# Windowed attention and a gated layer on one core: queries loaded a token to a partition and transposed by transfers, half a tile per step

## The chip, the cores and the metric

The kernel runs on one core of a Trainium2 chip. A core has a matrix engine (TensorE, in the profile PE, with its weight loads as PEld), a vector engine (DVE), a scalar engine (ACT), a general engine (GpSimd, POOL) and a sync engine (SP) that mainly issues transfers. Each engine works through its own instructions in the order of the program and waits on semaphores for the others. Transfers (DMA) are issued from the queues of SP, ACT and POOL and run on sixteen DMA engines. The metric is the device time of one execution in microseconds, as the median of several; less is better.

## The reference

```python
# q, k, v: (8, 8, 576, 64) float32 = batch, heads, tokens, head size
scores = (1 / sqrt(64)) * q @ k.T                 # per batch and head
mask   = abs(pos_q - pos_k) <= 32                 # within one batch entry
attn   = softmax(where(mask, scores, -1e9))
x      = (attn @ v) -> (4608 tokens, 512)         # heads side by side
h      = x @ w_in                                 # 512 -> 2048
g      = h * sigmoid(1.702 * h)
out    = g @ w_out                                # 2048 -> 512, float32
```

## The kernel before

The 8 x 576 tokens are treated as one row of 4608. Attention runs over 36 units of 128 queries: unit u holds the queries 128u+32 to 128u+159, in two blocks of 64, and each block sees 128 keys that start 32 tokens before it. The two layers run over 18 tiles of 256 tokens (two units). `head` starts up and works on tokens 0 to 1535; after it `window(w)` is called for w = 4 to 19. A window w computes the attention of units 2w and 2w+1, the first layer of tile w-1 (eight steps of eight matmuls, `layer1`), and the second layer of tile w-2 by seven products of 2x2 blocks (`product`). The order of all instructions on every engine is written out by hand.

Scores need keys and queries with the head dimension on the partitions. They stand in `kT` and `qT`, rings of 1536 tokens, of which each tile of 512 tokens (0 to 8) fills a third. A few tokens behind the end of each ring repeat its beginning, so that a block that crosses the end can be read in one piece. Tiles get into the rings in several ways:

- Tiles A (320 tokens) and B (256), 1, 2 and 3: `load_heads` loads four consecutive tokens of a head to a partition (256 numbers in a row). `pair_heads` copies them on DVE or POOL so that two heads stand side by side, TensorE transposes them through PSUM (`heads_T`, L176 and L179), and DVE (keys, `keys_T`) or ACT (queries, `queries_T`) copies the result to the ring (L106).
- Keys of tiles 4 to 8: `load_keys` (L146) loads one token to a partition (rows of 64 numbers), and `keys_X` (L151) writes the ring by a transposing transfer on SP, 128 tokens each.
- Queries of tiles 4 to 8: `load_heads` as above, four copies on DVE (`pair_heads`), and one transposing transfer for all 512 tokens (`queries_X`, L221).

Because of the four tokens to a partition, `qT` keeps queries in the order (token modulo 4, token divided by 4). A block of 64 queries is therefore four runs of 16, and the exponential (L269) writes its 64 results back in natural order.

The loads are issued on POOL's queue (they cast float32 to bf16). In `window`, `loads()` comes first: two loads of values `ve` (L157), which wait until the buffers of eight units earlier are free, and in even windows the keys and queries of tile w/2+3. `feed(w)` comes near the end: the shifted values `vo` (`odd_v`), and the transposing transfers; in even windows the first half of the keys of tile w/2+2, in odd ones the queries and the second half of the keys of tile (w+4)/2 rounded down. On SP's queue they stand between the stores of the output (L423, L349) and the transposing transfers of the attention's result, `x_T` to `xT` (L315), which the first layer of the next window reads. In window 4 TensorE transposes tile 3 between the last four steps of `layer1`; this is the only window in which it transposes keys or queries.

The casting loads of POOL and the transfers of SP each cycle through eight semaphores. A transfer that takes a semaphore again waits until the one before it on that semaphore has landed, so at most eight loads and eight SP transfers are under way.

Of the kernel before, what the change touches and what calls it, by code (L numbers as in the profile page):

```python
# [16 lines left out]
BF16 = mybir.dt.bfloat16  # L17
# [7 lines left out]
RING = 1536  # L25
RP = RING // JT


class _Kernel:
# [37 lines left out]
    def setup(self):  # L67
        nc, cst = self.nc, self.cst
        self.ident = cst.tile([128, 128], BF16, name="ident")
        self.mask = cst.tile([128, 4, SQ], BF16, name="mask")  # L70
        self.w_in_sb = cst.tile([128, self.NK, self.DFF], BF16, name="w_in_sb")
        self.w_out_sb = cst.tile([128, self.NFF, self.DM], F16, name="w_out_sb")
        self.w_sum = cst.tile([128, 4, self.NFF // 2, self.DM // 2], F16, name="w_sum")
        self.kT = cst.tile([128, 4, RING + 64], BF16, name="kT")
        self.qT = cst.tile([128, 4 * JT, RP + 16], BF16, name="qT")
        self.k_first = cst.tile([128, 4, 64], BF16, name="k_first")
        self.q_first = cst.tile([128, 4 * JT, 8], BF16, name="q_first")
        self.ve = [cst.tile([128, self.H, 66], BF16, name=f"ve{i}") for i in range(NV)]
        self.vo = [cst.tile([128, self.H, 66], BF16, name=f"vo{i}") for i in range(NV)]
        self.v_first = cst.tile([64, self.H, 66], BF16, name="v_first")  # L80
        self.idle = cst.tile([128, 512], BF16, name="idle")
        nc.vector.memset(self.idle, 0.0)
        self.spark = cst.tile([128, 1], F32, name="spark")
        nc.vector.memset(self.spark, 0.0)
        make_identity(nc, self.ident)
        for i in range(NV):
            nc.vector.memset(self.ve[i][:, :, self.D:], 1.0)
# [52 lines left out]

    def load_keys(self, i):

        kn = self.stage["k", i] = self.work.tile([128, JT, self.H, self.D], BF16, name="ks", tag="ks", bufs=3)
        for c in range(JT):
            for off, b, s, n in self.pieces(512 * i + 128 * c, 128):
                self.nc.gpsimd.dma_start(kn[off:off + n, c], self.k[b, :, s:s + n, :].rearrange("h s d -> s h d"))  # L146

    def keys_X(self, i, c):

        at = (512 * i + 128 * c) % RING  # L150
        self.nc.sync.dma_start_transpose(self.kT[:, :, at:at + 128],  # L151
                                         self.stage["k", i][:, c].rearrange("p h d -> p (h d)"))

# [28 lines left out]

    def keys_T(self, i, hp, kind="t", eng=None):
        tp = self.heads_T("k", i, hp, kind)
        lo, size = self.tokens(i)
        at = lo % RING

        def put(dst, n):
            self.cast(eng or self.nc.vector, dst.rearrange("r (p j) -> r p j", j=JT),
                      tp[:, :, :n // JT].rearrange("r j p -> r p j"))  # L190

        put(self.kT[:, hp, at:at + size], size)
        if at == 0 and lo:
            put(self.kT[:, hp, RING:], 64)

    def queries_T(self, i, hp, kind="t", eng=None):
        lo, size = self.tokens(i)
        at, n = lo // JT % RP, size // JT
        tp = self.heads_T("q", i, hp, kind)
        self.cast(eng or nc.vector, self.qT[:, JT * hp:JT * hp + JT, at:at + n], tp[:, :, :n])  # L200

# [16 lines left out]

    def queries_X(self, i):
        at = (128 * i) % RP  # L220
        self.nc.sync.dma_start_transpose(self.qT[:, :, at:at + 128],  # L221
                                         self.stage["q", i, "c"].rearrange("p h j t d -> p (h j t d)"))

    def queries_wrap(self, i):
        if (128 * i) % RP == 0:
            self.nc.vector.tensor_copy(self.qT[:, :, RP:RP + 8] if i else self.q_first, self.qT[:, :, 0:8])

    def setup_neg(self):

        pool = self.nc.gpsimd  # L230
        self.neg = self.cst.tile([128, 2, SQ], BF16, name="neg")
        pool.memset(self.neg, 0.0)
        for b in range(2):
            for half in range(2):
                sign = 1 if half == b else -1
                ap = self.neg[64 * half:64 * half + 64, b, :].rearrange("k (j s) -> k j s", j=JT)
                pool.affine_select(out=ap, in_=ap, compare_op=ALU.is_ge, fill=-30000.0, base=0,  # L237
                                   pattern=[[-sign, JT], [-sign * JT, SQ // JT]], channel_multiplier=sign)

# [8 lines left out]
    def scores(self, u):  # L248
# [6 lines left out]
        for hp in range(4):  # L255
            for blk in range(2):
                k0 = (128 * u + 64 * blk) % RING
                q0 = (128 * u + 64 * blk + 32) % RING // JT
                for half in range(2):
                    lo, at = 64 * half, k0 + 64 * (half ^ blk)  # L260
                    for eo in range(2):
                        r = slice(eo * 64, eo * 64 + 64)
                        nc.tensor.matmul(sc[eo][lo:lo + 64, 2 * hp + blk, :], self.kT[r, hp, at:at + 64],  # L263
                                         self.qT[r, JT * hp:JT * hp + JT, q0:q0 + 16], start=(seen and n == 0),
                                         stop=(n == 7), skip_group_check=not seen)
                n += 1
        p = self.work.tile([128, 2, 8, SQ], BF16, name="p", tag="p", bufs=5)
        for eo in range(2):
            nc.scalar.activation(p[:, eo].rearrange("k h (s j) -> k h s j", j=JT),  # L269
                                 sc[eo].rearrange("k h (j s) -> k h s j", j=JT), AF.Exp, scale=self.scale)  # L270
        self.p[u] = p
# [168 lines left out]
    def head(self):  # L440
# [37 lines left out]
        for hp in range(4):  # L478
            self.keys_T("A", hp, "ht"[hp % 2], dve)
            self.queries_T("A", hp, "ho"[hp % 2], act)  # L480
            if hp < 2:
                self.blind(hp)
# [21 lines left out]
        for hp in range(4):  # L504
            self.keys_T("B", hp, "htho"[hp], dve)
            if hp < 2:
                self.pair_heads("q", "B", hp + 2, dve)
            self.queries_T("B", hp, "hoth"[hp], act)
        self.scores(2)
# [14 lines left out]
        dve.tensor_copy(self.k_first, self.kT[:, :, 0:64])  # L524
        self.queries_wrap(0)
        for n in range(4):
# [13 lines left out]
        for hp in range(4):  # L540
            self.keys_T(1, hp, "a", dve)
            self.queries_T(1, hp, "a", act)
            run(1)
# [27 lines left out]
        for c in "kq":  # L571
            self.load_heads(3, c)
        self.layer1(2, 0)
# [8 lines left out]
        for hp in range(4):  # L582
            self.keys_T(2, hp, "t", dve)
            if hp in (1, 2):
                self.w_sums(hp + 1, 1)
            self.queries_T(2, hp, "o", act)
            self.layer1(2, 4 + hp)
        for m in (7, 8, 9):
            self.odd_v(m, dve)
        for m in (11, 12, 13):  # L590
            self.load_v(m)
        self.load_keys(4)
        self.load_heads(4, "q")

    def window(self, w):
# [10 lines left out]
        def loads():  # L606
            for m in (2 * w + 6, 2 * w + 7):
                if m < self.NU:
                    self.load_v(m)
            if w % 2 == 0 and 512 * (w // 2 + 3) < self.N:  # L610
                self.load_keys(w // 2 + 3)
                self.load_heads(w // 2 + 3, "q")

        if w == 4:
# [9 lines left out]
            self.gelu_table()  # L624
            for m in (10, 11):
                self.odd_v(m, act)
            self.band(b)
# [11 lines left out]
            loads()  # L639
            run(l1, 2)  # L640
            for c in "qk":
                for hp in range(4):
                    self.pair_heads(c, 3, hp, dve)
            run(l1, 2)
            for hp in range(4):
                self.keys_T(3, hp)
                self.queries_T(3, hp, "a", nc.scalar)
                run(l1)
            self.g_sums(w - 1, 0)
# [79 lines left out]
    def feed(self, w):  # L729

        dve = self.nc.vector
        if w % 2 == 0:
            self.queries_wrap((w + 2) // 2)
        for m in (2 * w + 2, 2 * w + 3):
            if 11 < m < self.NU:
                self.odd_v(m, dve)
        i = (w + 4) // 2
        if 512 * i < self.N:
            if w % 2:
                if 512 * i % RING == 0:  # L740
                    dve.tensor_copy(self.kT[:, :, RING:], self.kT[:, :, 0:64])
                for hp in range(4):
                    self.pair_heads("q", i, hp, dve)
                self.queries_X(i)
            for c in ((2, 3) if w % 2 else (0, 1)):
                self.keys_X(i, c)
        if w == 16:
            dve.tensor_copy(self.kT[:, :, RING:], self.k_first)
            dve.tensor_copy(self.qT[:, :, RP:RP + 8], self.q_first)

# [51 lines left out]
```

## Time and profile before

| | |
|---|---|
| time, median of 8 runs | 299.08 us (295.73 to 302.59) |
| the profiled execution | 296.16 us, of which its span is 294.0 us |
| granted clock of TensorE | 0.999 |
| packets of the casting loads (software queue) | 75,888, 18.16 MB |
| packets of SP's queue | 42,272, 18.62 MB |
| packets under 512 B, of all 118,649 | 96,080 |
| POOL's issues of query loads | 17, of 64 to 512 KB |
| POOL's issues of key loads | 30, most of 128 KB |
| SP's transposing transfers | 28 to `xT`, 20 to `kT`, 5 to `qT` |

Lines of the profile read `line engine operation out<-in shapes xcount | busy us, mean ns | idle before`. Lines of the timeline read `start us, us, engine line operation xcount [idle before <- what ended it]`; consecutive alike instructions are merged, and a q behind an engine's name means its queue (an issue or a wait, during which the engine itself does nothing). "DMA to landing" is the time from the issue of a transfer to the semaphore that tells of its end.

### The profile page before, as it was taken

Reading aid. Unit: us, or ns where it says so; the run is one execution under the profiler, and the core shown is the slowest. Engines: PE = TensorE matmul, PEld = TensorE weight load, DVE = VectorE, ACT = ScalarE, POOL = GpSimd, SP = SyncE. Lnnn points to the kernel's source line nnn. Section 1 sums busy time; section 2 is a strip of 40 time slices with the busy share of each in tenths; the row PEclk is TensorE's granted clock in tenths of the full one; section 3 lists DMA queues with packets and bytes.
Section 4 is the critical chain, followed back from the end, with each engine's and each line's share of the span. In section 5 each row is a group of like instructions: output and inputs, shape, how many; then the busy total and the mean of one; then the engine's idle time right before and its main releaser. Section 6 shows DMA issues by size and latency. Waiting matters only on the chain.

```text
span 294.0 us, 9589 instructions
## 1 busy us (share of the span) xinstructions
PE 287.4 (98%) x4052; PEld 236.4 (80%) x4052; DVE 193.8 (66%) x584; ACT 189.6 (64%) x314; POOL 87.3 (30%) x127
## 2 busy tenths in 40 slices
PE   8999999999999999999999999999999999999994
PEld 3568765865888888888888888888888888888884
DVE  3652467678696857685868586858685858583352
ACT  4676547688775757575757575757575757575330
POOL 8875533987457102720252020202000000000000
PEclk9999999999999999999999999999999999999999
DMA  8999999999999998999299929690963030303012
GB/s 144 149 204 207 200 184 167 160 167 184 139 164 163 174 149 149 152 193 169 66 166 196 192 27 140 112 179 8 139 117 100 12 101 16 97 14 95 2 71 71
DMA packets 118649, 37.76 MB, mean 128 GB/s; under 512 B 96080, under 2 KB 114256, under 8 KB 118608
## 3 DMA queue, kind: packets, MB, share of 16 engines
q0 software_dynamic: 75888, 18.16, 73.6%
q1 hardware_dynamic: 42272, 18.62, 31.9%
q8 instruction: 31, 0.51, 0.7%
q10 hardware_dynamic: 448, 0.39, 0.5%
q14 instruction: 10, 0.08, 0.1%
HBM read 36.96 MB, written 9.44 MB: 158 GB/s over the span
## 4 chain that ended last, share of the span: by engine, by line
PE 92%; DMA 3%; POOL 3%; DVE 1%; issue 0%; ACT 0%; POOLq 0%; DVEq 0%
PE h_ps L332 43%; PE o_ps L394 32%; PE o_ps L344 7%; PE pv L292 4%; PE sc L263 4%; DMA w_in_sb<-in_moe_w_in_dram 3%; PE tp L176 2%; POOL ve L157 1%; PE tp L319 0%; POOL qs L138 0%; POOL ks L138 0%; DVE o_sb L412 0%; POOL neg L237 0%; DVE part L106 0%; ACT o_sb L106 0%
## 5 line engine op out<-in xcount | busy, mean ns | idle before, releaser
L332 PE MATMUL h_ps<-xT,w_in_sb 128*128 128x256 bf16 x1152 | 135.8, 273 | 0.4 <-DMA w_in_sb<-in_moe_w_in_dram 0.3
L334 ACT ACTIVATE g<-h_ps 128x512 f16<-128x512 f32 x144 | 85.6, 595 | 73.5 <-PE h_ps L332 72.1
L332 PEld LDWEIGHTS <-w_in_sb 128*128 128x128 bf16 x1152 | 111.9, 98 | 13.9 <-DMA w_in_sb<-in_moe_w_in_dram 0.4
L157 POOL DMA_DIRECT2D ve<-in_v_dram x40 | 34.0, 858 | 97.2 <-PE pv L292 79.0
L394 PEld LDWEIGHTS <-gs 128*128 128x128 f16 x480 | 45.8, 98 | 5.8
L394 PE MATMUL o_ps<-w_sum,gs 128*128 128x256 f16 x360 | 44.3, 273 | 0.0
L269 ACT ACTIVATE p<-sc 128x512 bf16<-128x512 f32 x72 | 37.2, 603 | 2.7 <-PE sc L263 2.5
L394 PEld LDWEIGHTS <-g 128*128 128x128 f16 x360 | 34.1, 98 | 4.6 <-ACT g L334 0.2
L371 DVE TENSOR_TENSOR gs<-g 128x512 f16<-128x512 f16 x30 | 12.6, 422 | 31.6 <-ACT g L334 31.6
L304 DVE TENSOR_TENSOR x<-pv,rec 128x256 bf16<-128x256 f32 x72 | 30.5, 424 | 2.7 <-DVE rec L303 0.3
L394 PE MATMUL o_ps<-w_out_sb,g 128*128 128x256 f16 x240 | 29.0, 273 | 0.0
L412 DVE TENSOR_TENSOR o_sb<-o_ps,part 128x256 f32<-128x256 f32 x45 | 19.0, 422 | 12.1 <-PE o_ps L394 11.4
L106 DVE COPY part<-o_ps 128x256 f32<-128x256 f32 x45 | 19.1, 424 | 11.7 <-PE o_ps L394 10.3
L281 DVE TENSOR_TENSOR p<-p,mask 128x512 bf16<-128x512 bf16 x64 | 24.4, 423 | 0.8 <-ACT p L269 0.7
L344 PE MATMUL o_ps<-w_out_sb,g 128*128 128x512 f16 x96 | 23.2, 380 | 0.0
L106 DVE COPY vo<-ve 64x528 bf16<-64x528 bf16 x61 | 18.6, 305 | 3.3 <-DMA ve<-in_v_dram 2.0
L146 POOL DMA_DIRECT2D ks<-in_k_dram x22 | 18.9, 874 | 2.1 <-DMA qs<-in_q_dram 1.0
L269 ACT ACT_TABLE_LOAD x15 | 19.2, 1283 | 0.3
L431 ACT ACT_TABLE_LOAD x15 | 19.2, 1283 | 0.3
L303 DVE RECIPROCAL rec<-pv 128x4 f32<-128x4 f32 x72 | 12.6, 175 | 10.2 <-PE pv L292 10.2
L106 DVE COPY kT<-tp 128x512 bf16<-128x512 bf16 (+3 forms) x24 | 12.2, 529 | 6.3 <-PE tp L176 5.9
L292 PEld LDWEIGHTS <-p 128*64 128x64 bf16 x576 | 11.1, 110 | 6.1 <-DVE p L281 3.6
(69 smaller groups left out, 263.2 us busy)
## 6 DMA issues: line engine op xcount, KB each, us to landing
out_dram<-o_sb SPq DMA_DIRECT2D x34, 256.0 KB, 3.0
ve<-in_v_dram POOLq DMA_DIRECT2D x32, 128.0 KB, 6.4
ks<-in_k_dram POOLq DMA_DIRECT2D x19, 128.0 KB, 8.1
w_in_sb<-in_moe_w_in_dram POOLq DMA_DIRECT2D x4, 512.0 KB, 11.4
w_out_sb<-in_moe_w_out_dram POOLq DMA_DIRECT2D x4, 512.0 KB, 12.1
qs<-in_q_dram POOLq DMA_DIRECT2D x2, 448.0 KB, 11.2
qs<-in_q_dram POOLq DMA_DIRECT2D x3, 256.0 KB, 7.2
qs<-in_q_dram POOLq DMA_DIRECT2D x2, 384.0 KB, 11.2
```

The source lines that it names most:

```text
L106: (eng.copy if eng is self.nc.scalar else eng.tensor_copy)(out, in_)
L157: self.nc.gpsimd.dma_start(self.ve[m % NV][off:off + n, :, :self.D], self.v[b, :, s:s + n, :].rearrange("h s d -> s h d"))
L269: nc.scalar.activation(p[:, eo].rearrange("k h (s j) -> k h s j", j=JT), sc[eo].rearrange("k h (j s) -> k h s j", j=JT), AF.Exp, scale=sel ...
L281: self.nc.vector.tensor_mul(pv, pv, msk.to_broadcast([128, 4, 2, SQ]))
L292: nc.tensor.matmul(acc[half][blk * 64:blk * 64 + 64, hh, :], p[:, h % 2, h // 2 * 2 + blk, :], vt[:, h, :D + 1], start=(hh == 0), stop=(hh ...
L304: nc.vector.tensor_mul(x[:, hs, :], acc[half][:, :, :D], rec[:, hs, :].to_broadcast([128, 4, D]))
L332: nc.tensor.matmul(hps[:, i, :], self.w_in_sb[:, kr, ff * 128:(ff + 1) * 128], self.xT[t][:, kr, :], start=(i == 0 and kr == 0), stop=(i = ...
L334: nc.scalar.activation(self.g[t][:, ffs[0]:ffs[1] + 1:ffs[1] - ffs[0], :], hps, AF.Gelu_apprx_sigmoid)
L344: nc.tensor.matmul(o_ps, self.g[t][:, ff, s * 128:(s + 1) * 128], self.w_out_sb[:, ff, :], start=(ff == 0), stop=(ff == self.NFF - 1))
L394: nc.tensor.matmul(self.part[t, key], x, y, start=(first and k == 0), stop=(k == 7), skip_group_check=True)
L412: self.nc.vector.tensor_add(dst, self.part[t, src], self.part[t, other])
L431: self.nc.scalar.activation(self.spark, self.spark, AF.Gelu_apprx_sigmoid)
```

## The change

The queries take the path that the keys of tiles 4 to 8 took, and both take it from tile 3 on.

- `qT` keeps queries in natural order. The scores read 64 queries in one run, the exponential is a plain one, and the additive mask `neg` is built without the reordering. For tiles A, B, 1 and 2 ACT's copy from PSUM to `qT` reads with a stride, as DVE's copy to `kT` does.
- `load_rows` loads keys and queries one token to a partition, for chosen quarters of a tile (128 tokens, 128 partitions x 8 heads x 64 numbers); `rows_X` transposes them by one transfer for each quarter. A query tile is so loaded as rows of 64 numbers where it was rows of 256, and by four transposing transfers where it was one. `queries_X`, `queries_wrap` and DVE's copies before them are gone.
- Tile 3 is no longer transposed by TensorE: 32 transposes, 8 copies by `pair_heads`, 8 copies by DVE and 4 by ACT go from window 4. Its loads (two halves) and the transfers of its first half are in `head`.
- Loads and transfers go in halves: each window loads two quarters of keys and two of queries of tile w/2+2, and each `feed` transposes two of each. The loads of a tile are issued one to two windows later than before, in smaller portions.
- `odd_v(10)` and `odd_v(11)` move from ACT to DVE, and behind the attention of window 4.

```diff
-        self.qT = cst.tile([128, 4 * JT, RP + 16], BF16, name="qT")
+        self.qT = cst.tile([128, 4, RING + 32], BF16, name="qT")
...
+    def load_rows(self, c, i, chunks):
+        key, src = (c, i), {"q": self.q, "k": self.k}[c]
...
+        for n in chunks:
+            for off, b, s, m in self.pieces(512 * i + 128 * n, 128):
+                self.nc.gpsimd.dma_start(self.stage[key][off:off + m, n], src[b, :, s:s + m, :].rearrange("h s d -> s h d"))
+
+    def rows_X(self, c, i, chunks):
+        dst = {"q": self.qT, "k": self.kT}[c]
+        for n in chunks:
+            at = (512 * i + 128 * n) % RING
+            self.nc.sync.dma_start_transpose(dst[:, :, at:at + 128],
+                                             self.stage[c, i][:, n].rearrange("p h d -> p (h d)"))
...
     def scores(self, u):
...
-                                         self.qT[r, JT * hp:JT * hp + JT, q0:q0 + 16], start=(seen and n == 0),
+                                         self.qT[r, hp, q0:q0 + SQ], start=(seen and n == 0),
...
-            nc.scalar.activation(p[:, eo].rearrange("k h (s j) -> k h s j", j=JT),
-                                 sc[eo].rearrange("k h (j s) -> k h s j", j=JT), AF.Exp, scale=self.scale)
+            nc.scalar.activation(p[:, eo], sc[eo], AF.Exp, scale=self.scale)
...
     def head(self):
...
         for c in "kq":
-            self.load_heads(3, c)
+            self.load_rows(c, 3, (0, 1))
...
         for m in (11, 12, 13):
             self.load_v(m)
-        self.load_keys(4)
-        self.load_heads(4, "q")
+        for c in "kq":
+            self.load_rows(c, 3, (2, 3))
+        for c in "kq":
+            self.rows_X(c, 3, (0, 1))
...
     def window(self, w):
...
-            if w % 2 == 0 and 512 * (w // 2 + 3) < self.N:
-                self.load_keys(w // 2 + 3)
-                self.load_heads(w // 2 + 3, "q")
+            i, chunks = w // 2 + 2, ((0, 1), (2, 3))[w % 2]
+            if 512 * i < self.N:
+                for c in "kq":
+                    self.load_rows(c, i, chunks)
...
         if w == 4:
...
-            for m in (10, 11):
-                self.odd_v(m, act)
...
-            run(l1, 2)
-            for c in "qk":
-                for hp in range(4):
-                    self.pair_heads(c, 3, hp, dve)
-            run(l1, 2)
-            for hp in range(4):
-                self.keys_T(3, hp)
-                self.queries_T(3, hp, "a", nc.scalar)
-                run(l1)
+            for m in (10, 11):
+                self.odd_v(m, dve)
+            run(l1, 8)
...
     def feed(self, w):
-        if w % 2 == 0:
-            self.queries_wrap((w + 2) // 2)
...
-        i = (w + 4) // 2
+        i = (w + 3) // 2
         if 512 * i < self.N:
-            if w % 2:
-                if 512 * i % RING == 0:
-                    dve.tensor_copy(self.kT[:, :, RING:], self.kT[:, :, 0:64])
-                for hp in range(4):
-                    self.pair_heads("q", i, hp, dve)
-                self.queries_X(i)
-            for c in ((2, 3) if w % 2 else (0, 1)):
-                self.keys_X(i, c)
+            if w % 2 == 0 and 512 * i % RING == 0:
+                dve.tensor_copy(self.kT[:, :, RING:], self.kT[:, :, 0:64])
+                dve.tensor_copy(self.qT[:, :, RING:], self.qT[:, :, 0:32])
+            for c in "kq":
+                self.rows_X(c, i, ((2, 3), (0, 1))[w % 2])
```

## The prediction

> **What bounds the kernel now.** I read the page's busy row and the chain that ended last, then the timeline of the stretch that the change edits, then the table by windows, and last the transfers.
>
> ```profile
> PE 287.4 (98%) x4052; PEld 236.4 (80%) x4052; DVE 193.8 (66%) x584; ACT 189.6 (64%) x314; POOL 87.3 (30%) x127
> ...
> PE 92%; DMA 3%; POOL 3%; DVE 1%; issue 0%; ACT 0%; POOLq 0%; DVEq 0%
> ```
>
> TensorE is busy for 98% of the span and is 92% of the chain that ended last. Nothing but TensorE's own work, or a new wait of TensorE, can move the time. In window 4 the timeline of TensorE reads:
>
> ```profile
> 75.20 0.39 PE L176 MATMUL tp<-ident,kc 128*128 128x128 bf16 x4
> 75.43 0.39 PE L176 MATMUL tp<-ident,qc 128*128 128x128 bf16 x4
> 75.65 1.04 PE L332 MATMUL h_ps<-xT,w_in_sb 128*128 128x256 bf16 x8
> 76.52 0.39 PE L176 MATMUL tp<-ident,kc 128*128 128x128 bf16 x4
> ```
>
> One round is 4 transposes of keys, 4 of queries and one step of the first layer: 75.20 to 76.52, 1.32 us, four times. In a stretch without transposes the chain has 48 such matmuls, six steps:
>
> ```profile
> 90.21 5.24 PE h_ps L332 x48
> ```
>
> so a step alone takes 5.24 / 6 = 0.87 us. The steady windows are equal, whether they carry much load traffic (the second) or little:
>
> ```profile
> 95.40:110.00 14.60, 14.60 (x221) 12.78 (x220) 10.88 (x35) 9.87 (x16) 1.77 (x2) 1.00 1.71 163
> 110.00:124.60 14.60, 14.60 (x217) 12.78 (x216) 10.12 (x32) 9.87 (x16) 7.59 (x10) 1.00 1.21 148
> ```
>
> Columns: stretch, length, busy us of PE, PEld, DVE, ACT, POOL, granted clock, DMA share, GB/s. TensorE fills all of both; DVE and ACT have 3.7 us or more to spare. What TensorE could come to wait for is `xT`, which SP transposes behind its other transfers:
>
> ```profile
> 90.19 1.43 SPq L315 DMA_TRANSPOSE xT<-x  x1
> 91.72 0.72 SPq L423 DMA_DIRECT2D out_dram<-o_sb  x1
> 96.34 5.66 SPq L221 DMA_TRANSPOSE qT<-qc  x1
> 102.09 4.37 SPq L151 DMA_TRANSPOSE kT<-ks  x2
> 106.55 1.22 SPq L315 DMA_TRANSPOSE xT<-x  x1
> 107.87 0.52 SPq L423 DMA_DIRECT2D out_dram<-o_sb  x1
> 108.48 1.23 SPq L315 DMA_TRANSPOSE xT<-x  x1
> ```
>
> The view of the tile `xT`, asked for the issue at 90.19 alone and for that at 108.48 alone, gives the landings:
>
> ```profile
> DMA to landing us min/median/max: 8.5/8.5/8.5
> ...
> DMA to landing us min/median/max: 5.3/5.3/5.3
> ```
>
> The first lands at 98.7 and is read by the step that starts at 99.55: 0.9 us to spare. The second lands at 113.8 for a step at 114.16: 0.4 us. These two margins are the narrowest in the kernel. For window 5 (issue 72.48, landing after 8.8, step at 84.94) it is 3.7 us, from window 8 on some 3 us.
>
> **The change part by part.**
>
> *TensorE.* The 32 transposes of tile 3 go: 4 rounds x (1.32 - 0.87) = 1.8 us, all on the chain. The row of L176 (48 in 4.6 us busy) would make it 32 x 96 ns = 3.1 us, but busy time counts each transpose's tail, which overlaps the next; the spacing of the starts decides: 1.8 us. The eight steps then follow each other. ACT keeps pace: it takes 0.60 us per step and shows 0.28 us idle before each.
>
> *Scores and exponential.* 64 score matmuls take 0.67 us from their start at 109.99 to the next product at 110.66, 10.5 ns each, on quarters of the array (64 columns each). The value matmuls read plain runs of 65 numbers on halves of it and take 0.64 us for 32, 20 ns each: twice the time at half the parallelism, so the strided query read costs nothing that I can see. I take 0 (ends: 0 and a tenth of 1152 x 10.5 ns, a gain of 1.2 us). The exponential with the strided read of PSUM takes 603 ns, the plain gelu of equal size 595: 0. For the same reason I take 0 for ACT's twelve copies to `qT` that now read with a stride (581 ns for 512 numbers today, 584 for its plain copy to `xT`). DVE does lose by a stride, 690 against 418 ns. If ACT did so too, tile B's four copies (374 ns) would grow by about 0.24 us each; scores 2 and 3, which read them, end 0.3 us before TensorE waits for `w_in_sb` at 18.8, so at worst some 0.6 us would show.
>
> *DVE and ACT.* DVE loses 8 + 20 `pair_heads` (about 0.30 us each, 8.5 us), four copies of 0.69 and four of 0.21 (3.6 us), and gains four `odd_v` copies (1.2 us). ACT loses four of those (630 ns, 2.5 us) and four copies (2.3 us). All lies beside TensorE's work: 0. The `odd_v` pair on DVE waits for values 11 and 12, which landed at 67.5 and 69.1 and now come behind more loads; DVE reaches it at 72.1 (the end of the last `x` of window 4) and has slack there, since its copies and transposes of tile 3 are gone until `g_sums` at about 79. Behind it wait `g_sums` and the two copies to the rings' ends.
>
> *Waits that are new.* These two copies wait for the first transfers of tile 3. Loads: POOL issues three values at 53.50 and then six loads where it had four, at 0.7 to 0.9 us each, to 60.7. Nine loads of up to 1024 rows are 7168 rows; at the rate found below they land by about 64. SP then issues four transposes at 1.2 us (median of L151), up to 2.6 under load, to about 70, and they land within 9 us, by 74 to 79; DVE reaches the copies at 79 to 80. Cover of 0 to 5 us. Behind the copies are the additions and `keep` of window 5; each microsecond too late would cost up to one. On SP's queue the store of unit 4 (67.52) and `xT` of units 8 and 9 (71.08, 72.48) now stand behind these four. Should they go out 1.5 us late, window 5 still has 3.7 - 1.8 = 1.9 us to spare. I take 0.
>
> *Transfers.* A query tile of 512 tokens was 1024 rows of 512 B and becomes 4096 rows of 128 B (sizes as written). The key loads show both prices. The stretch 66 to 70, nearly only 128 B rows, moves 156 GB/s; the stretch 156 to 157.5, only the 512 B rows of the last query tile, 200 GB/s. 524 KB so cost 3.4 us in place of 2.6: 0.8 us more of DMA time per tile. Two windows (29.2 us) had 8 portions of 131 KB of keys and values (0.84 us each, 6.7), one query tile (2.6), 12 portions of 131 KB transposed (about 0.7 each at the 170 to 241 GB/s of stretches with transposes alone, 8.4), and four stores (262 KB at 237 GB/s, 1.1 each, 4.4): 22.1 us. After: 22.9 us. The DMA engines keep room.
>
> A rule speaks against this. The Trainium skill, "DMA: Bandwidth & Descriptors", Specifications, wants at least 512 B per transfer for line rate, and says that below it the engine reads, modifies and writes. If a 128 B row cost as much as one of 512 B, the query tile would take 4 x 2.6 = 10.4 us, and two windows 29.9 of 29.2 us: DMA-bound, with `xT` late every time. The trace has the key rows of 128 B at 156 GB/s, where this would give 50; I take the trace, and keep the rule for the second rival.
>
> *Queues.* Per two windows SP issued one `qT` (median 3.0 us, longest 5.7) and four `kT` (1.2): 7.9 us. Now it is eight at 1.2: 9.8 us, spread evenly. The long stop from 91.7 to 106.5 (wait for DVE's copies, then `qT`, then `kT`), which leaves `xT` its 0.4 us, goes: four issues of 1.2 to 2.6 us right after the store at 91.7 end by about 102 at worst, when the next `x` is due. Against that, each window now has 4 transposes and 6144 load rows, where even and odd windows had 2 and 6 portions transposed and 7168 and 2048 rows. POOL issues six loads of 0.88 us a window, 5.3 of 14.6 us.
>
> *Sum.* -1.8 us, and 0 for the rest: 296.2 - 1.8 = 294.4 for an execution like the profiled one. That one lies 2.9 us under the median of the eight; against the median, 299.1 - 1.8 = 297.3 us.
>
> **The rivals.**
>
> *1. More than the transposes goes.* The runs spread over 6.9 us, while the profiled one has hardly a gap on TensorE. If the slower ones lose their time where `xT` has 0.4 and 0.9 us to spare, and SP's stop at 91.7 to 106.5 is gone, most would come near the fast end: 299.1 - 1.8 - (1 to 3) = 294.3 to 296.3 us. For it: the margins. Against: no trace shows a slow run, and the variation may lie outside the kernel. 0.26.
>
> *2. `xT` late in every window: slower.* In windows 5 to 13 each `xT` now meets load traffic. It has 9.4 us from its issue (90.19) to its use (99.55); under load it took 8.5 to 9.0 in windows 4 and 5, and 6.3 in a loaded window at 119.4. If landing takes 10 us, TensorE waits 0.6 us a window, 5 us in nine; that is where it decides, above 9.4 us plus a fifth of a microsecond per window to pay back the 1.8. By the rule above it is +0.7 us per two windows for the DMA alone, and worse behind it. Net +3 to +6: 302 to 305 us. Against it: the sum of 22.9 of 29.2 us, and that the loaded windows of today are no longer than the others. 0.27.
>
> *3. The gain is eaten in windows 5 and 6.* Four more transposes by tile 3, 0.9 us of margin in window 6, and ring copies with a cover of perhaps 0: one stall of 1 to 2 us. 298 to 300 us. 0.17.
>
> *Forecast as summed.* 297.3, its own range 296 to 298.5. 0.30.
>
> **How the numbers follow.** The likeliest single case is the sum: 297.3 us. About 1%, 3 us, is what a measurement of this kernel tells from no change. Faster by that (under 296.1): most of rival 1 and a little of the sum, 0.29. Slower (over 302.1): most of rival 2, 0.26. Within: 0.45. The range leaves out the far half of rival 2 and the best tenth: 294.0 to 303.0 us.
>
> **What would show it.** Right: in window 4 eight steps at 0.87 us with no transposes, the windows after it at 14.6 us with TensorE full, query rows at some 150 GB/s, and `xT` landing within 9 us. Wrong: TensorE idle before L332's counterpart with DMA as its releaser (rival 2), or DVE waiting for a transfer at the ring copies (rival 3). A DMA rate under 100 GB/s beside the new loads would overthrow the price of the rows; the score matmuls at another spacing, the zero for the strided read.

## The result and the profile after

| | before | after |
|---|---|---|
| time, median | 297.02 us (59 executions) | 294.5 us (22) |
| ratio after / before, 95% interval | | 0.992 (0.990 to 0.994) |
| profiled execution | 296.16 us, span 294.0, clock 0.999 | 295.45 us, span 293.7, clock 0.994 |
| span, median of the executions (of all comparisons) with a granted clock of 0.997 or more | 294.2 us (30) | 292.3 us (22) |
| time less span, median of the same | 1.92 us | 1.72 us |

The forecast was 297.3 us within 294.0 to 303.0; the time is 294.5. The kernel is 2.5 us faster where 1.8 was forecast, 0.8%, which is less than the 1% that the forecast called a difference. Most of the distance to 297.3 is the level: the median of 299.08 over eight executions became 297.02 over 59. Some executions of a kernel fall into a slower state; the ratios, and the times of the experiments below, leave these out.

The two profiled spans can't be compared as they stand. TensorE ran at half clock for 3.4 us from 19.2 us in the profiled execution of after, and its first matmuls came later. So I compare single stretches of the traces, and spans only where the clock is alike.

The page of after, its busy row, its two large queues (packets, MB, share of 16 engines) and the chain that ended last:

```profile
PE 286.7 (98%) x4020; PEld 235.4 (80%) x4020; DVE 187.8 (64%) x552; ACT 185.3 (63%) x306; POOL 104.0 (35%) x146
...
q0 software_dynamic: 97696, 18.16, 84.6%
q1 hardware_dynamic: 47104, 19.67, 39.9%
...
PE 92%; DMA 3%; POOL 3%; DVE 1%; issue 0%; ACT 0%; POOLq 0%; DVEq 0%
```

TensorE still fills the span and still makes the chain. The casting loads now take 84.6% of the engines' span in place of 73.6%, with the same bytes, and from window 4 on TensorE waits for none of them. The timeline of TensorE in window 4 of after:

```profile
72.79 1.03 PE L325 MATMUL o_ps<-w_out_sb,g 128*128 128x512 f16 x4
73.65 7.16 PE L313 MATMUL h_ps<-xT,w_in_sb 128*128 128x256 bf16 x64
80.74 0.45 PE L245 MATMUL sc<-qT,kT 64*64 64x64 bf16 x32
```

The eight steps are one row: 64 matmuls without a transpose between them. From the last scores of window 4 to the first of window 5 before took 65.35 to 80.58, 15.23 us, and after 67.50 to 80.74, 13.24 us: 1.99 us less, of which 1.8 are the transposes. The other 0.2 us are seen in before, in the timelines of ACT and of TensorE:

```profile
68.59 2.59 ACT L106 COPY vo<-ve 64x528 bf16<-64x528 bf16 x4
71.09 0.57 ACT L106 COPY xT<-tp 128x512 bf16<-128x512 bf16 x1
...
70.64 1.03 PE L344 MATMUL o_ps<-w_out_sb,g 128*128 128x512 f16 x4
71.71 3.65 PE L332 MATMUL h_ps<-xT,w_in_sb 128*128 128x256 bf16 x32
```

ACT was still in `odd_v(10)` and `odd_v(11)` when TensorE had finished transposing the `x` of unit 7 (70.41 to 70.80). Its copy to `xT` began at 71.09, and the first step at 71.71, 1.07 us after the start of the four products before it. In after the same distance is 73.65 - 72.79 = 0.86 us. The pair of `odd_v` had moved to DVE.

The windows after it (columns as in the forecast), and the landing times of eleven transfers to `xT` issued from 74.5 to 148.9 us in after:

```profile
95.54:110.16 14.62, 14.62 (x219) 12.80 (x218) 10.31 (x30) 9.87 (x16) 6.26 (x8) 1.00 1.80 149
124.85:139.46 14.61, 14.61 (x218) 12.80 (x217) 10.15 (x31) 9.87 (x16) 5.26 (x6) 1.00 1.89 166
...
DMA to landing us min/median/max: 5.4/7.7/8.4
```

14.6 us, TensorE full, as before, and 149 to 166 GB/s beside the new loads, where under 100 would have overthrown the price of the rows. SP's queue and DVE's copies to the rings' ends in after:

```profile
90.36 1.34 SPq L296 DMA_TRANSPOSE xT<-x  x1
91.79 0.55 SPq L404 DMA_DIRECT2D out_dram<-o_sb  x1
92.44 2.63 SPq L154 DMA_TRANSPOSE kT<-ks  x2
95.16 4.53 SPq L154 DMA_TRANSPOSE qT<-qs  x2
102.29 1.20 SPq L296 DMA_TRANSPOSE xT<-x  x1
104.55 0.33 SPq L404 DMA_DIRECT2D out_dram<-o_sb  x1
104.97 1.32 SPq L296 DMA_TRANSPOSE xT<-x  x1
...
79.45 0.22 DVE L714 COPY kT<-kT 128x256 bf16<-128x256 bf16 x1
79.59 0.19 DVE L715 COPY qT<-qT 128x128 bf16<-128x128 bf16 x1
```

The long stop of SP from 91.7 to 106.5 is gone: the queue is free at 99.7, and `xT` is issued as soon as its `x` is there (102.29). The second transfer to `xT` (104.97) landed after 7.9 us, at 112.9, for a step at 114.41: 1.5 us to spare, where before had 0.4. That of 90.36 landed after 7.4 us for a step at 99.72: 2.0 us, where before had 0.9. The copies show no wait; the first transfers of keys and queries, which they read, had landed by 73.4.

### The profile page after: what moved, and what is told of

Its sections match the earlier page's. It is cut to its first block, busy times and chain, and to the rows that moved or that the text cites. A ratio compares the mean times of both kernels' runs of the same rounds, so it can differ in the third digit from the quotient of the medians.

```text
span 293.7 us, 9542 instructions
## 1 busy us (share of the span) xinstructions
PE 286.7 (98%) x4020; PEld 235.4 (80%) x4020; DVE 187.8 (64%) x552; ACT 185.3 (63%) x306; POOL 104.0 (35%) x146
## 3 DMA queue, kind: packets, MB, share of 16 engines
q0 software_dynamic: 97696, 18.16, 84.6%
## 4 chain that ended last, share of the span: by engine, by line
PE 92%; DMA 3%; POOL 3%; DVE 1%; issue 0%; ACT 0%; POOLq 0%; DVEq 0%
PE h_ps L313 43%; PE o_ps L375 32%; PE o_ps L325 7%; PE pv L273 4%; PE sc L245 4%; DMA w_in_sb<-in_moe_w_in_dram 3%; POOL ve L160 1%; PE tp L179 1%; PE tp L300 0%; POOL qs L137 0%; POOL ks L137 0%; DVE o_sb L393 0%; POOL neg L219 0%; DVE part L105 0%; ACT o_sb L105 0%
## 5 line engine op out<-in xcount | busy, mean ns | idle before, releaser
L315 ACT ACTIVATE g<-h_ps 128x512 f16<-128x512 f32 x144 | 85.7, 595 | 74.9 <-PE h_ps L313 73.6
L105 DVE COPY part<-o_ps 128x256 f32<-128x256 f32 x45 | 19.1, 424 | 12.6 <-PE o_ps L375 11.2
L147 POOL DMA_DIRECT2D qs<-in_q_dram x27 | 22.8, 863 | 5.3 <-DMA ks<-in_k_dram 4.1
L147 POOL DMA_DIRECT2D ks<-in_k_dram x27 | 22.8, 857 | 3.4 <-DMA ve<-in_v_dram 2.2
L105 DVE COPY vo<-ve 64x528 bf16<-64x528 bf16 x65 | 20.2, 311 | 2.0 <-DMA ve<-in_v_dram 0.5
L251 ACT ACT_TABLE_LOAD x15 | 19.2, 1283 | 0.3
L412 ACT ACT_TABLE_LOAD x15 | 19.2, 1283 | 0.3
```

Of the source, the lines that this page charges most:

```text
L105: (eng.copy if eng is self.nc.scalar else eng.tensor_copy)(out, in_)
L147: self.nc.gpsimd.dma_start(self.stage[key][off:off + m, n], src[b, :, s:s + m, :].rearrange("h s d -> s h d"))
L251: nc.scalar.activation(p[:, eo], sc[eo], AF.Exp, scale=self.scale)
L315: nc.scalar.activation(self.g[t][:, ffs[0]:ffs[1] + 1:ffs[1] - ffs[0], :], hps, AF.Gelu_apprx_sigmoid)
L412: self.nc.scalar.activation(self.spark, self.spark, AF.Gelu_apprx_sigmoid)
```

## The experiments

Eleven kernels ran. Ratios are to the kernel before on the same chip, with 95% intervals.

| run | what differs | time | ratio |
|---|---|---|---|
| e1_tile3_pe | after, tile 3 on TensorE | 297.31 | 1.001 (0.998 to 1.004) |
| e2_tile3_only | before, tile 3 by the old transfers | 304.44 | 1.025 (1.020 to 1.029) |
| e3_oddv_act | after, `odd_v` pair on ACT | 293.15 (one) | |
| e4_more_128 | after, more rows of 128 B | 294.99 | 0.993 (0.990 to 0.996) |
| e5_more_512 | after, the same bytes in rows of 512 B | 296.32 | 0.997 (0.993 to 1.001) |
| e6_tile2_too | after, tile 2 by transfers too | 301.8 | 1.015 (1.011 to 1.020) |
| e7_late_x3 | after, first half of tile 3 late | 302.31 (one) | |
| e8_twice_128 | after, four more portions per window | 305.13 | 1.027 (1.022 to 1.032) |
| e9_half | before, only keys of tile 3 by transfers | 302.61 | 1.016 (1.011 to 1.022) |
| e10_tile2_keys | after, keys of tile 2 by transfers too | 294.87 | 0.995 (0.991 to 0.999) |
| e11_after_again | after | 293.95 | 0.993 (0.990 to 0.995) |

### Is the gain tile 3's? (e1, e3)

e1 puts tile 3 back on TensorE and keeps the rest of the change:

```diff
-            run(l1, 8)
+            run(l1, 2)
+            for c in "qk":
+                for hp in range(4):
+                    self.pair_heads(c, 3, hp, dve)
+            run(l1, 2)
+            for hp in range(4):
+                self.rows_T("k", 3, hp, "t", dve)
+                self.rows_T("q", 3, hp, "a", act)
+                run(l1)
```

> The changed kernel with one part undone: tile 3 is again loaded four tokens to a partition and transposed by TensorE in window 4; all later query tiles keep the new path. Theory (the gain is TensorE's 32 transposes and the ACT copies in window 4): window 4 grows back from 13.2 to about 15.0 us between its last scores and those of window 5, and the time is that of the kernel before, 297.0 us, to within 0.5 us (ratio 0.998 to 1.002). Rival 1 (the smoother SP queue gives a part of the gain in the windows after): a gain of 0.6 us or more stays, ratio 0.998 or less.

No gain is left: 1.001. TensorE's timeline in e1:

```profile
71.70 3.66 PE L313 MATMUL h_ps<-xT,w_in_sb 128*128 128x256 bf16 x32
76.04 0.40 PE L179 MATMUL tp<-ident,kc 128*128 128x128 bf16 x4 [0.68 <-DVE kc L105]
76.28 0.39 PE L179 MATMUL tp<-ident,qc 128*128 128x128 bf16 x4
76.50 1.04 PE L313 MATMUL h_ps<-xT,w_in_sb 128*128 128x256 bf16 x8
```

The transposes are back, with a wait of 0.68 us for DVE, which in this order does `odd_v` first. So e1 is a little worse than before in window 4 (16.1 us against 15.23) and before's equal in time. At a clock of 0.997 or more its span is 294.9 us against 294.35 for before on the same chip, 0.55 us more where window 4 alone has 0.9: natural order, the strided copies and the new load pattern by themselves change the span by no more than some tenths.

e3 puts only the pair of `odd_v` back on ACT, ahead of `x_T(7)`:

```diff
+            for m in (10, 11):
+                self.odd_v(m, act)
...
-            for m in (10, 11):
-                self.odd_v(m, dve)
```

> The changed kernel with the shifted values 10 and 11 back on ACT at their old place in window 4. Theory: ACT's copy of xT for unit 7 comes late again, and the first layer-one matmul of window 4 starts about 0.4 us after the instruction before it, waiting for ACT, where the changed kernel has 0.1 to 0.2: 0.2 us, to be seen in the timeline alone. Rival: the wait does not come back, and the 0.2 us of the changed kernel have another cause.

TensorE's timeline in e3:

```profile
70.03 1.03 PE L325 MATMUL o_ps<-w_out_sb,g 128*128 128x512 f16 x4
71.11 7.15 PE L313 MATMUL h_ps<-xT,w_in_sb 128*128 128x256 bf16 x64
```

The gap ahead of the first step comes back (1.08 us between the two starts, 0.86 in after), and window 4 takes 13.43 us (64.75 to 78.18) against 13.24. The whole time can't show 0.2 us: the one execution lies inside after's own spread.

### Would the old form do for tile 3? (e2, e9)

e2 takes before, and brings tile 3 in by the old transfers: keys by quarters, queries by one transfer of the whole tile.

```diff
-        for c in "kq":
-            self.load_heads(3, c)
+        self.load_keys(3)
+        self.load_heads(3, "q")
...
+        for c in (0, 1):
+            self.keys_X(3, c)
...
-                self.keys_T(3, hp)
-                self.queries_T(3, hp, "a", nc.scalar)
-                run(l1)
+                self.pair_heads("q", 3, hp, dve)
+            self.queries_X(3)
+            for c in (2, 3):
+                self.keys_X(3, c)
+            run(l1, 8)
```

> The kernel before with one part of the change alone: tile 3 goes the way of tiles 4 to 8 (keys a token to a partition, queries four tokens to a partition, four copies on DVE, one transposing transfer), so that TensorE's 32 transposes go from window 4, and nothing else of the queries changes; the shifted values 10 and 11 stay on ACT. Theory: 1.8 us less than before, ratio 0.994, with window 4 at 13.4 us and a rest of 0.2 us of waiting before its first layer-one step. Rival (the new query path is needed for the gain, since the transposing transfer of a whole query tile blocks SP): the gain is lost again to a late xT in windows 5 to 7, ratio 0.998 or more.

It missed by 3%. The transposes are gone, and two waits stand in their place. In e2, first TensorE's timeline, then that of SP, that of ACT, and the view of waits (waiting instruction <- what it waited for: us in total, times, longest):

```profile
74.44 7.15 PE L332 MATMUL h_ps<-xT,w_in_sb 128*128 128x256 bf16 x64 [1.63 <-ACT xT L106]
90.12 0.59 PE L263 MATMUL sc<-qT,kT 64*64 64x64 bf16 x28 [6.15 <-DVE qT L226]
...
75.64 7.96 SPq L221 DMA_TRANSPOSE qT<-qc  x1
...
71.85 2.06 ACT L106 COPY vo<-ve 64x528 bf16<-64x528 bf16 x3 [1.48 <-DMA ve<-in_v_dram]
...
DVE qT L226 <- DMA qT<-qc: 9.6, 1, 9.6
```

The transfer of the whole tile went out at 75.64, behind DVE's copies and SP's transfers of `xT`, took SP 7.96 us to issue and landed at 89.85. DVE stood 9.6 us at the ring copy, and the scores of unit 11 behind it waited 6.15 us. And `odd_v(11)` on ACT waited for a value that came later behind the tile's loads, with `xT` queued behind it: 1.63 us. The granted clock was half from 86.4 to 93.2. After has transfers of quarter tiles in place of this, the first of them in `head`: e7 below tests the place, no run tests the size alone. `odd_v` on ACT is not what decides: in e3, behind after's loads, it costs 0.2 us.

e9 moves only the keys (16 of the 32 transposes), and `odd_v` to DVE:

```diff
-        for c in "kq":
-            self.load_heads(3, c)
+        self.load_keys(3)
+        self.load_heads(3, "q")
...
+            for m in (10, 11):
+                self.odd_v(m, dve)
...
-                self.keys_T(3, hp)
```

> The kernel before with the keys of tile 3 alone on the path of tiles 4 to 8, half of them transposed by transfers that are issued in the head, its queries still transposed by TensorE in window 4, and the shifted values 10 and 11 on DVE. 16 of the 32 transposes go. Theory (each group of four transposes is worth 0.22 us of TensorE's chain, and the late ACT copy 0.2): 0.9 + 0.2 = 1.1 us less than before, ratio 0.996, window 4 at 14.1 us. Rival: something of the new query path is needed, and there is no gain, ratio 0.999 or more.

Window 4 did as expected: 14.13 us against 15.23, 0.9 for the transposes and 0.2 for the copy. The loss comes three windows later, in window 7. TensorE and SP in e9:

```profile
111.84 1.91 PE L394 MATMUL o_ps<-w_sum,gs 128*128 128x256 f16 x16
118.02 1.86 PE L332 MATMUL h_ps<-xT,w_in_sb 128*128 128x256 bf16 x8 [4.28 <-DMA xT<-x]
...
96.09 5.72 SPq L221 DMA_TRANSPOSE qT<-qc  x1
101.90 2.61 SPq L151 DMA_TRANSPOSE kT<-ks  x2
104.60 2.34 SPq L315 DMA_TRANSPOSE xT<-x  x1
```

This is the narrowest margin of before, the `xT` issued at 108.48, which landed after 5.3 us with 0.4 to spare. In e9 it went out at 107.68 and landed after 10.2 us. In before the ten loads of windows 5 and 6 had been issued from 84.6 to 93.4 and had landed by 106.5, so that `xT` met no more than two loads of values; in e9 they went out from 89.7 to 101.6 and landed up to 119.8, so that it met them. Why POOL ran those 5 to 8 us later I read only from the longer landings ahead of them and tried no further. So rival 2's mechanism is real under the old queue order, with one `xT` late, not nine.

### Is the cover of the ring-end copies real? (e7)

```diff
# end of head
-        for c in "kq":
-            self.rows_X(c, 3, (0, 1))
# window 4, before run(l1, 8)
+            for c in "kq":
+                self.rows_X(c, 3, (0, 1))
```

> The changed kernel with the first half of tile 3's transposing transfers issued behind the transfers of xT in window 4 (some 76 to 81 us) instead of in the head (65 to 69 us). The prediction's step that the ring-end copies are covered (6.2 us of cover in the changed kernel) says: that cover is used up, the last of the four lands near 88 us, VectorE waits for it at its two copies (79.5 us) for 4 to 8 us, and the scores of units 10 and 11 that follow are late by 1 to 5 us: a span of 293 to 297 us, 1 to 4 us over the changed kernel's 291.3 to 293.6. If the moment of issue in the head doesn't matter, no wait shows at the two copies and the span is the changed kernel's own.

DVE and TensorE in e7:

```profile
84.18 0.23 DVE L714 COPY kT<-kT 128x256 bf16<-128x256 bf16 x1 [6.59 <-DMA kT<-ks]
87.00 0.20 DVE L715 COPY qT<-qT 128x128 bf16<-128x128 bf16 x1 [2.59 <-DMA qT<-qs]
...
87.25 0.59 PE L245 MATMUL sc<-qT,kT 64*64 64x64 bf16 x28 [6.00 <-DVE qT L715]
87.78 3.60 PE L375 MATMUL o_ps<-w_sum,gs 128*128 128x256 f16 x16
```

The wait falls where it was expected, at the two copies, and takes 9.2 us of DVE and 6.0 us of TensorE. The span was 300.6 us, above the 293 to 297 expected: the wait alone was longer, and from 86.2 on the granted clock was half for 6.8 us (16 products in 3.60 us, which take 1.92 at full clock). The cover is needed; the place of issue in `head` is part of the gain.

### How much room do the transfers have? (e4, e5, e8)

e4 adds four unread portions of 131 KB in rows of 128 B to every second window from 4 to 12, e5 the same bytes in rows of 512 B, e8 four portions to every window from 4 to 13:

```diff
+            if w % 2 == 0 and w < 13:
+                extra = self.work.tile([128, JT, self.H, self.D], BF16, name="qc", tag="qc")
+                for n in range(JT):
+                    self.nc.gpsimd.dma_start(extra[:, n], self.q[0, :, 128 * n:128 * n + 128, :].rearrange("h s d -> s h d"))
```

> The changed kernel with 524 KB more to load in every second window from 4 to 12, as four portions of rows of 128 B (a query tile's worth, in the new form), into a buffer that nothing reads. The load work of two windows rises by the price of a query tile in the new form, 3.4 us, to about 26.3 of 29.2 us. Theory (the trace's price of such rows): the DMA engines still keep up, the windows stay at 14.6 to 14.7 us, and the time is that of the changed kernel, 294.5 us, to +1.5. Rival 2 (a row of 128 B costs as much as one of 512 B): 10.4 us more in two windows, far over 29.2; the windows from 5 to 13 take 16 us and more, over 305 us.

> The same 524 KB in every second window, but as one load with rows of 512 B, the old form of a query tile. Theory: 2.6 us of DMA work, 0.8 us less than with rows of 128 B; the time is that of the changed kernel to +1.5 us and within 1 us of the run with rows of 128 B. Rival 2: the same here, but several us under the run with rows of 128 B.

> The changed kernel with four portions of rows of 128 B more in every window from 4 to 13, twice the extra load of the other run. By the trace's prices the DMA work of two windows is 22.9 + 6.8 = 29.7 us in 29.2: over the edge. Theory: TensorE now waits for xT in several of the windows 6 to 13, which stretch by 0.3 to 1 us each: 297 to 304 us. If the sum has the DMA work too high, the windows stay at 14.6 us and the time at 294.5 to 295.5; if it is far too low, they stretch by more than 2 us each, over 312 us.

e4 does as expected: at a clock of 0.997 or more its median span is 293.05 us against 292.2 for after on the same chip (e11). e5 misses its expectation, with 294.4: 2.2 us over after where at most 1.5 was expected, and 1.3 over e4. Its 524 KB came as one load, not as four, and I did not follow where it loses; but rows of 512 B bring no advantage, and the fourfold price of short rows, which would have put e4 over 305 us, is refuted. With e8 the edge is passed. A stretch of e4 and its longest stop, then of e8 the windows 9 and 10, and TensorE in the latter:

```profile
109.60:124.20 14.60, 14.60 (x219) 12.78 (x216) 10.14 (x31) 9.74 (x17) 5.37 (x7) 1.00 2.10 151
...
202.77 0.19 PE L273 MATMUL pv<-vo,p 128*64 128x65 bf16 x1 [1.11 <-issue]
```

```profile
137.20:151.81 14.61, 14.61 (x217) 12.80 (x216) 10.60 (x31) 9.87 (x16) 9.99 (x13) 1.00 2.45 140
151.81:169.18 17.37, 14.93 (x218) 12.79 (x217) 10.70 (x31) 9.98 (x16) 8.99 (x11) 1.00 1.85 154
...
152.72 0.41 PE L245 MATMUL sc<-qT,kT 64*64 64x64 bf16 x28 [0.43 <-DMA qT<-qs]
158.74 1.03 PE L313 MATMUL h_ps<-xT,w_in_sb 128*128 128x256 bf16 x8 [2.01 <-DMA xT<-x]
```

By the forecast's prices two windows hold 22.9 us of transfers in after, 22.9 + 4 x 0.84 = 26.3 in e4, and 29.6 in e8, of 29.2. In e4 TensorE never waits for `xT`; only windows 11 and 13 are longer than after's, 15.05 and 15.91 us, the latter by a stop for which the trace names no releaser. e8 waits, from window 10 on, once a backlog has built up: its windows 10 to 14 take 15.2 to 19.1 us, and half clock follows two of the waits. Three of them stretch by 2.8 to 4.5 us, more than the 0.3 to 1 expected, and 305.1 us lies over the 297 to 304. The edge lies between these two loads, as the forecast's prices have it; e4's two longer windows say that it is not sharp.

### Can more be had the same way? (e6, e10, e11)

e6 brings all of tile 2 in by transfers, e10 its keys alone:

```diff
# e10
-        for c in "kq":
-            self.load_heads(2, c)
+        self.load_rows("k", 2, range(4))
+        self.load_heads(2, "q")
...
+        self.rows_X("k", 2, range(4))
...
-            self.rows_T("k", 2, hp, "t", dve)
```

> The changed kernel taken one tile further: tile 2 too is loaded a token to a partition and transposed by SP, so that its 32 transposes on TensorE, its copies on DVE and ACT and the eight copies on POOL in the head go. Theory: another 4 x 0.45 = 1.8 us from TensorE's chain, ratio to before 0.986, if tile 2 lands and is transposed before scores 7 and 8 at about 61 us. Rival (the loads of the head are already bound by the transfers up to 48 us, and 12 transposes stand behind each other on SP): scores 7 or 8 wait for the rings, or xT of units 8 and 9 is late, and the time is that of the changed kernel or up to 5 us more, ratio 0.992 to 1.01.

> The changed kernel with the keys of tile 2 (not its queries) also by transposing transfers in the head. Theory: TensorE loses 16 more transposes, 0.9 us, and these four transfers, issued between 53 and 60 us, land by 69 us, where the scores of unit 8 need the first of them at 66 to 68 us: 0.9 us faster than the changed kernel if they are in time, a ratio to the kernel before of 0.988 to 0.990. Rival: the head's transfers set the end already, as with keys and queries of tile 2 (1.0152): the scores of unit 8 wait 1 to 4 us and TensorE then runs at half clock for 3 to 7 us, a ratio of 0.996 to 1.01.

> The changed kernel once more, beside the kernel before and the other two on the same chip. Theory (transposes 1.8 us, a copy of xT no longer late 0.2 us, time outside the span 0.2 us): 2.0 to 2.4 us faster, a ratio of 0.992 to 0.9935. If more than that goes (rival 1), 0.988 or less.

TensorE in e6, then in e10:

```profile
64.70 0.58 PE L245 MATMUL sc<-qT,kT 64*64 64x64 bf16 x32 [4.73 <-DMA qT<-qs]
67.95 0.59 PE L245 MATMUL sc<-qT,kT 64*64 64x64 bf16 x28 [2.67 <-DMA qT<-qs]
68.47 4.33 PE L325 MATMUL o_ps<-w_out_sb,g 128*128 128x512 f16 x12
```

```profile
63.00 0.65 PE L245 MATMUL sc<-qT,kT 64*64 64x64 bf16 x36
64.98 0.41 PE L245 MATMUL sc<-qT,kT 64*64 64x64 bf16 x28 [1.32 <-DMA kT<-ks]
```

In e6 the scores wait 7.4 us in all for an expected gain of 1.8 us, and from 64.8 to 71.7 the clock is half (the 12 products of 4.33 us take 2.76 at full clock). In e10 the stretch with the transposes is 0.44 us shorter (13.90 against 14.34), and the scores of unit 8 then wait 1.3 us. Its executions at clock 0.997 or more have a median span of 293.0 us against 292.2 for after on the same chip: no gain. And five of its 12 executions had a clock of 0.981 to 0.989, as e6's all had, and took 298.2 to 301.2 us; of after's 29 none was below 0.994. The rival of both was right: in `head` the transfers are the limit. e11 repeats after at 0.993, where 2.0 to 2.4 us were expected (0.992 to 0.9935). No version that ran beats after.

## Why the prediction was right, point by point

- **TensorE, 1.8 us.** Right, and read rightly from the spacing of the starts: 1.99 us went from the stretch, of which 1.8 are the transposes and 0.2 the item below. The busy time of the transposes would have promised 3.1.
- **"DVE and ACT ... All lies beside TensorE's work: 0."** Mis-sized by 0.2 us. The forecast asked what DVE loses by taking `odd_v`, not what stood behind `odd_v` on ACT: the copy of unit 7's `xT`, which TensorE's first step waited for. e3 brings the 0.2 us back.
- **The sum was made against the span, with what lies around it unchanged.** At like clock that remainder was 1.92 us before and 1.72 after, another 0.2 us. All eleven kernels of the experiments have it at 1.70 to 1.76 (medians), e1 with tile 3 on TensorE and e2 and e9 with the old query path among them. So it follows none of the parts that these runs separate; what makes it is open, and it need not be the change. Span and remainder together are 296.09 - 294.02 = 2.1 us at like clock (medians of the times).
- **The rest of the 2.5 us** may come from the mix of executions: granted clocks of 0.993 to 0.996 (1.4 to 1.6 us longer) were seen in 20 of 52 executions before and 7 of 29 after; in the profile of after it is the half clock from 19.2 us on. Whether the change has a part in that is open.
- **The level.** 299.08 us was the median of eight executions that lay high; the 297.3 inherits it. That, not the mechanism, is 2.1 of the 2.8 us between forecast and time. It was in part luck that the time lies inside the range, 0.5 us from its end: only rival 1, whose reason did not show, had carried the range so far down.
- **Scores, exponential and strided copies, 0.** Right: in after 64 scores still take 0.67 us, the exponential 603 ns, ACT's strided copies to `qT` 583 ns (374 for tile B's). The loss that DVE has by a stride ACT has not. e1, with all of these and tile 3 on TensorE, has before's time.
- **Ring-end copies, cover 0 to 5 us.** Sized too low: the cover was 6.2 us in after's trace (79.59 - 73.4), and e7 shows that it is real: without it TensorE stands for 6.0 us.
- **Transfers, 22.9 of 29.2 us.** Right, within what e4 and e8 tell: no `xT` late at 26.3, several waits at 29.6. Short rows are dearer by 156 against 200 GB/s, as the forecast read them in before, and not fourfold. Had a row of 128 B cost as much as one of 512 B, after itself would have been at 29.9 and slower, and e5 far faster than e4.
- **Rival 1, more than the transposes goes.** Its size came nearest in the time (294.3 to 296.3), but its reason did not show: with SP's stop gone and tile 3 on TensorE, e1 is no faster. At like clock 0.3 us went beyond the 1.8, no more than the two items of 0.2 us.
- **Rival 2, `xT` late.** Landing took 5.4 to 8.4 us in the eleven cases above, against 9.4 us where it decides. It does happen, in one window, in e9's queue order, and in after under e8's load.
- **Rival 3, windows 5 and 6.** Did not happen: the margin in window 6 grew from 0.9 to 2.0 us and that in window 7 from 0.4 to 1.5, as the forecast had it for SP's stop.

## What to carry to other kernels

When work is taken off the engine that bounds a kernel, its worth is the spacing of the starts with and without it, not its busy time; but whether it shows depends on when its replacement lands. The same removal of transposes was worth 2 us where the first transfers were issued 14 to 17 us ahead of their reader. Against the kernel before it cost 5 to 7 us where the queries came in one late transfer of the whole tile (e2), where the first transfers were issued late (e7), or where half of the removal left the tightest old transfer in a busier stretch (e9). When an instruction moves from one engine to another, ask on both sides: who waits behind it where it arrives, and who was waiting behind it where it leaves.

## What the runs showed of the hardware

- A wait of TensorE costs more than itself. With waits of 6.2 us (e2), 6.0 (e7), 4.3 (e9) and 4.7 (e6) the granted clock was half for 6.8 us, which began between 3.7 us before the end of the wait (e2) and 0.1 us after it (e6). In e8 waits of 1.9 and 2.8 us were followed by 3.4 us at half clock each, while the one of 2.0 us shown above was not. The expectation for e7 left this out. The Trainium skill, "TensorE: Matmul & The Clock Gate", What's actually happening, names a window of about 3.4 us of idleness after which the clock falls, and the stretches of 3.4 and 6.8 us fit one and two such windows; but by it neither wait in e8 would have brought one, and the measurement decides.
- The landing time of a load grows with the queue ahead of it, and by itself does not tell whether TensorE waits. Between 66 and 230 us the casting loads, of 131 KB mostly, landed in after with medians of 6.2 us (values) to 9.5 (queries), from 3.7 to 15.0 in all; in e4 the medians were 14.3 to 14.7 us, and no `xT` was late.
- In loaded windows one transposing transfer of 512 tokens held SP's queue for 5.7 to 8.0 us and landed after 12.2 to 14.2 us (before, e9, e2). In after the transfers of 128 tokens held it for 1.2 to 2.8 us each and landed after at most 9.7 us, with medians of 7.3 (keys) and 6.6 (queries).
